# A fused RWKV-6 scan and SiLU feed-forward kernel: ScalarE's part of a weight piece, the odd-key copies, masks and block loads in another order

## The chip, the cores and the metric

The kernel runs on one core of a Trainium2 chip. The metric is device time in microseconds (us). A core has five engines that run side by side, each with its own queue: TensorE (PE in the profile), VectorE (DVE), ScalarE (ACT), GpSimd (POOL) and SyncE (SP), which here issues almost all transfers. [...] In this kernel the program sets the order in each queue by the order in which it emits instructions; nothing is rescheduled.

## The reference

Two blocks follow each other. The first is an RWKV-6 attention with a decaying state for each head, over 4 batches, 8 heads, 768 tokens and head size 48; the second is a feed-forward block with SiLU, 3072 tokens, width 384, inner width 2048.

```python
# r, k, v, w: (B, H, S, D) = (4, 8, 768, 48); u: (H, D)
for t in range(S):
    cur = einsum('bhd,bhe->bhde', u[None] * k[:, :, t], v[:, :, t])
    y[:, :, t] = einsum('bhd,bhde->bhe', r[:, :, t], state + cur)
    state = w[:, :, t, :, None] * state + einsum('bhd,bhe->bhde', k[:, :, t], v[:, :, t])
x = y.transpose(0, 2, 1, 3).reshape(B * S, H * D)      # (3072, 384)
h = x @ w_in                                           # (384, 2048)
out = (h / (1 + exp(-h))) @ w_out                      # (2048, 384)
```

r, k, v, w and u come as 32-bit floats. The two weight matrices come as 64-bit floats, and the kernel turns them into 32-bit floats itself.

## The kernel before

The tokens are cut into 12 units of 128 tokens and two batches. The scan of one unit runs in 7 levels, in which blocks of 1, 2, 4 ... 64 tokens meet their neighbours. At each level TensorE computes scores from r and the keys; VectorE keeps the scores of the level through a mask and decays r; GpSimd decays the keys for the next level; ScalarE copies the odd key blocks, which the level leaves as they are.

```python
def level(i, l):
    c, ni = 1 << l, L >> (l + 1)
    x_at, next_at = X[l % 2], X[(l + 1) % 2]          # two places for the level's keys
    if l + 1 < NL:
        nc.scalar.copy(out=keys(next_at * L + c, ...), in_=keys(NP * L + c, ...))  # odd keys, L384
    sc = [ps.tile([128, Q, L // 2], F32, name=name, bufs=2) for e in range(2)]     # p_sc (or p_h in unit 0)
    for p in range(NP):
        for e in range(2):
            nc.tensor.matmul(...)                     # scores, L396: lhsT=tk at x_at, rhs=tr
    def keep(e): nc.vector.copy_predicated(out=score..., mask=masks[l]..., data=sc[e]...)   # L405
    if not alone:                                     # alone: unit 0
        keep(0); keep(1)
    if l + 1 < NL or units[i][0] > 0:
        nc.vector.tensor_tensor(out=rb..., in0=rb..., in1=t..., op=ALU.mult)       # decay of r, L414
    if alone:
        keep(0); keep(1)
    for b in range(NB):
        nc.gpsimd.tensor_tensor(out=out, in0=have, in1=odd, op=ALU.mult)           # key products, L434
    if i < NTOK:                                      # units 0 and 1
        product(i, l)                                 # GpSimd: decays of the next level, L338
    add_weight()                                      # GpSimd: add of a joined weight piece, L206
```

The 64-bit weights come in 16 pieces of 256 columns or rows (0 to 7: w_in, 8 to 15: w_out). ScalarE takes a head (L174, L180) and tails into PSUM (L178); VectorE joins them with the rest of the words (L194, L196); GpSimd adds head and low part into the 32-bit weight (L206). Head and low part have two buffers each, the tails two PSUM tiles `p_o`. Pieces are loaded into staging places that earlier pieces must have left.

```python
def split_weight(i):                                  # ScalarE
    nc.scalar.activation(out=upper, in_=staged(i)..., func=AF.Abs)                 # L174
    tails = [ps.tile([128, DM], F32, name="p_o", bufs=2) for x in range(PW // DM)]
    for x, tail in enumerate(tails):
        nc.scalar.activation(out=tail, ..., func=AF.Copy, scale=8.0)               # L178
    nc.scalar.activation(out=head, in_=upper.bitcast(U16), func=AF.Relu, ...)      # L180
def round_weight(i):
    add_weight()
    if rounded and 0 < i <= 2 * NW:
        join_weight(i - 1)                            # VectorE: four instructions
    if rounded and i < 2 * NW:
        split_weight(i)
    for j in due.get(i, ()):
        load_weight(j)
```

The other steps that the prediction speaks of are: `turn` (a unit's w, r or k transposed), `turn_k` (its final keys transposed; the ScalarE copies are `kq`), `y` (the unit's output; copies `yt`), `dense_x` (output to feed-forward input; copies `xt`), `update` (the state, with copies by VectorE), `up(i, m)` (one of 8 tiles of `x @ w_in` and its Silu; PSUM tile `p_h`, two buffers), `down` and `quarter` (products with w_out), `sums` (VectorE sums of up tiles), `bonus`, `bonus_sum` and `bonus_write` (the term with u, which VectorE writes into the scores with two large copies, L368), `beat(n)` (n transposes of the identity that nobody reads, which keep TensorE busy). The order in which the start emits them:

```python
do((beat, 14), *both(bonus, 0), *both(bonus_sum, 0), (bonus_write, 0),
   *both(turn, 0, "k"), (beat, 8), *both(turn, 0, "r"), (beat, 4), *both(turn, 0, "w"), (level, 0, 0), (clear_state,),
   (make_mask, 4), (beat, 8), (level, 0, 1), (make_mask, 5), (beat, 8), (level, 0, 2), (make_mask, 6), (beat, 8),
   (level, 0, 3), (reverse_v, 0), (round_weight, 0), (beat, 6), (level, 0, 4), (clear_tokens,), (beat, 6), (level, 0, 5),
   *both(turn, 1, "w"), (clear, 0), (level, 0, 6))
blocks = block_loads(2)
do(*both(turn, 1, "r"), *blocks[:8], *both(turn_k, 0), *both(y_state, 0), *both(y, 0), (round_weight, 1),
   *both(dense_x, 0), *both(turn, 1, "k"), (reverse_v, 1), (round_weight, 2))
blocks = [*blocks[8:], (clear, 1), *block_loads(3)]
others = {0: both(update, 0) + both(bonus, 1), 3: [(bonus_sum, 1, 0)], 4: [(bonus_sum, 1, 1)], 5: [(bonus_write, 1)],
          6: [(load_values, 2), (load_rk, 2)]}
for l in range(NL):
    do((level, 1, l), (round_weight, 3 + l), (up, 0, l), *others.get(l, ()), *blocks[l * 3:l * 3 + 3])
do((up, 0, 7), *both(y_state, 1), *both(y, 1), (round_weight, 10), *both(dense_x, 1), (round_weight, 11),
   *both(turn_k, 1), *both(turn, 2, "w"), (products, 2), *both(update, 1))
turns = {1: both(turn, 2, "k"), 2: both(turn, 2, "r"), 3: [(reverse_v, 2)], 5: [(sums, 1, 0)]}
for m in range(6):
    do((round_weight, 12 + m), (up, 1, m), *turns.get(m, ()))
# ... then for each level l of unit 2: (level, 2, l), down or up steps, bonus, sums, block loads;
# from unit 3 on a fixed mixture of one scan with the feed-forward of the two units before it
```

Of the kernel before, what the change touches and what calls it, by code (L numbers as in the profile page):

```python
# [8 lines left out]
F32 = mybir.dt.float32  # L9
# [25 lines left out]
def kernel(  # L35
# [115 lines left out]
    due = {r: [] for r in range(-1, 2 * NW + 1)}  # L151
    for i in range(2 * NW):
        due[max([j + 1 for j in range(i) if rounded and PLACES[j] == PLACES[i]], default=-1)].append(i)
# [16 lines left out]
    def split_weight(i):  # L170
# [3 lines left out]
        nc.scalar.activation(out=upper, in_=staged(i).bitcast(BF16)[:, 3::4], func=AF.Abs)  # L174

        tails = [ps.tile([128, DM], F32, name="p_o", bufs=2) for x in range(PW // DM)]
        for x, tail in enumerate(tails):
            nc.scalar.activation(out=tail, in_=staged(i).bitcast(U16)[:, 2::4][:, x * DM:(x + 1) * DM],  # L178
                                 func=AF.Copy, scale=8.0)
        nc.scalar.activation(out=head, in_=upper.bitcast(U16), func=AF.Relu, scale=8.0 * 2.0 ** 16, bias=shift)  # L180
        half[i] = head, tails

    def join_weight(i):
        head, tails = half.pop(i)
        lo, hi = staged(i)[:, 0::2], staged(i)[:, 1::2]
        dst = w_ends[i][0].bitcast(U32)
        low = temps[:, 2, i % 2]

        def like(t):
            return t.rearrange("p (c f) -> p c f", c=dst.shape[1])  # L190

        for x, tail in enumerate(tails):
            part = slice(x * DM, (x + 1) * DM)
            nc.vector.scalar_tensor_tensor(out=tail.bitcast(U32), in0=lo[:, part], scalar=2.0 ** -29, in1=tail,  # L194
                                           op0=ALU.mult, op1=ALU.add)
            nc.vector.scalar_tensor_tensor(out=low[:, part], in0=hi[:, part], scalar=0x80000000, in1=tail.bitcast(U32),  # L196
                                           op0=ALU.bitwise_and, op1=ALU.bitwise_or)
        joined.append((dst, like(head), like(low)))
# [8 lines left out]

    def round_weight(i):

        add_weight()  # L210
        if rounded and 0 < i <= 2 * NW:
            join_weight(i - 1)
        if rounded and i < 2 * NW:
            split_weight(i)
        for j in due.get(i, ()):
            load_weight(j)
# [507 lines left out]
```

## Time and profile before

| what | value |
|---|---|
| time, median of 3 runs | 711.57 us (710.77 to 712.9) |
| span of the profiled execution | 709.6 us |
| TensorE busy | 673.4 us, 95% |
| TensorE weight loads busy | 591.4 us, 83% |
| VectorE busy | 437.8 us, 62% |
| GpSimd busy | 263.0 us, 37% |
| ScalarE busy | 186.4 us, 26% |
| transfers | 49.03 MB, mean 69 GB/s |

A line of a group names the line of the kernel, the engine, the operation and what it writes and reads. A line of the waits names the waiting instruction, the one that released it, then the total in us, how often, and the longest. A line of the timeline has start, duration, engine, line, operation, and in brackets the idle time just before and what ended it. The granted clock is TensorE's, as a share of full speed.

The start of the page's view in 40 slices (each 17.7 us) shows where TensorE is not full:

```
PE   6877967999999999999999999999999999999998
DVE  6857866579665665665665665666666667564131
ACT  5476575112022022022022022022022022021020
POOL 8838554525415414414414414423423524220000
```

### The profile page before, as it was taken

The page shows a single profiled execution, that of the slowest core. Times are in us where ns is not written, and L with a number is a line of the kernel's source. Part 1 is how long each engine was busy: PE and PEld are TensorE (multiplying, and loading weights), DVE is VectorE, ACT ScalarE, POOL GpSimd, SP SyncE. Part 2 cuts the span into 40 slices and gives each one's busy share as a digit, 9 for nine tenths or more (in the row PEclk, how much of TensorE's full clock was granted, in tenths as well). Part 3 has the DMA queues.
Part 4 walks back from the last instruction along what each step waited for, and adds up shares of the span by engine and source line. Part 5 has one row for each costly group of instructions (what it writes and reads, how often), then busy time and mean ns, then how long its engine had stood idle before and what let it go on. Part 6 is the DMA issues. An engine that isn't in the chain of part 4 may idle for free. (4 is left out here: it accounts for less than half of the span.)

```text
span 709.6 us, 12908 instructions
## 1 busy us (share of the span) xinstructions
PE 673.4 (95%) x4910; PEld 591.4 (83%) x4910; DVE 437.8 (62%) x777; ACT 186.4 (26%) x380; POOL 263.0 (37%) x372
## 2 busy tenths in 40 slices
PE   6877967999999999999999999999999999999998
PEld 5765756668989989989989989989989989889997
DVE  6857866579665665665665665666666667564131
ACT  5476575112022022022022022022022022021020
POOL 8838554525415414414414414423423524220000
PEclk9898998999999999999999999999999999999999
DMA  9937672432531441541541541540540300100000
GB/s 212 244 46 206 129 151 116 75 54 51 94 53 32 93 57 28 95 57 26 98 58 28 95 58 27 95 59 26 96 60 22 81 1 23 46 1 20 26 0 23
DMA packets 224237, 49.03 MB, mean 69 GB/s; under 512 B 212016, under 2 KB 219056, under 8 KB 224176
## 3 DMA queue, kind: packets, MB, share of 16 engines
q1 hardware_dynamic: 224032, 48.02, 34.6%
q8 instruction: 39, 0.64, 0.4%
q10 hardware_dynamic: 144, 0.20, 0.1%
q14 instruction: 22, 0.18, 0.1%
HBM read 39.52 MB, written 4.72 MB: 62 GB/s over the span
## 5 line engine op out<-in xcount | busy, mean ns | idle before, releaser
L555 PE MATMUL p_h<-xt,w_in_sb 128*128 128x256 f32 x1152 | 271.3, 390 | 6.6 <-ACT gt L561 4.4
L555 PEld LDWEIGHTS p_h<-xt,w_in_sb 128*128 128x128 f32 x1152 | 217.5, 193 | 42.0 <-ACT gt L561 5.2
L434 POOL TENSOR_TENSOR tk<-tk,tw 128x256 f32<-128x256 f32 x168 | 121.0, 742 | 201.3 <-PE p_sc L396 125.0
L405 DVE COPY_PREDICATED score<-mask,p_sc 128x512 f32<-128x512 int8 x162 | 133.6, 891 | 99.8 <-PE p_sc L396 99.7
L561 ACT ACTIVATE gt<-p_h 128x512 f32<-128x512 f32 x93 | 55.1, 594 | 254.6 <-PE p_h L555 254.6
L396 PEld LDWEIGHTS p_sc<-tr,tk 48*128 48x128 f32 x1296 | 80.1, 188 | 35.3 <-issue 25.8
L396 PE MATMUL p_sc<-tr,tk 48*128 48x128 f32 x1296 | 95.8, 286 | 10.5 <-POOL tk L434 4.0
L613 PE MATMUL p_o<-w_out_sb,gt 128*128 128x192 f32 x528 | 91.4, 330 | 0.0
L613 PE MATMUL p_o<-own,temps 128*128 128x192 f32 x528 | 90.8, 329 | 0.0
L613 PEld LDWEIGHTS p_o<-own,temps 128*128 128x128 f32 x528 | 85.4, 190 | 3.3 <-DVE partial L620 2.2
L613 PEld LDWEIGHTS p_o<-w_out_sb,gt 128*128 128x128 f32 x528 | 85.4, 190 | 2.0 <-issue 0.4
L414 DVE TENSOR_TENSOR tr<-tr,tw 128x512 f32<-128x512 f32 x82 | 68.2, 832 | 2.1 <-issue 1.3
L384 ACT COPY tk<-tk 128x256 f32<-128x256 f32 x72 | 32.7, 454 | 126.0 <-PE p_sc L396 108.8
L338 POOL TENSOR_TENSOR tw<-tw 128x512 f32<-128x512 f32 (+6 forms) x84 | 40.2, 478 | 51.6 <-DVE tw L306 46.9
L487 POOL TENSOR_TENSOR state<-state,tw 128x512 f32<-128x512 f32 x16 | 16.6, 1061 | 92.7 <-PE p_m L457 92.7
L595 DVE TENSOR_TENSOR temps<-gt 128x256 f32<-128x256 f32 x88 | 39.2, 445 | 17.3 <-ACT gt L561 16.9
L622 DVE TENSOR_TENSOR ob<-p_o,partial 128x192 f32<-128x192 f32 x44 | 15.6, 354 | 46.4 <-PE p_o L613 46.3
L496 DVE TENSOR_TENSOR state<-p_sc,state 48x384 f32<-48x384 f32 x16 | 8.9, 555 | 40.5 <-PE p_sc L482 40.4
L368 DVE COPY_PREDICATED score<-own_mask,diag 128x1024 f32<-128x1024 int8 x24 | 32.2, 1397 | 0.5
L613 PE MATMUL p_o<-w_out_sb,temps 128*128 128x192 f32 x176 | 30.4, 326 | 0.0
L613 PEld LDWEIGHTS p_o<-w_out_sb,temps 128*128 128x128 f32 x176 | 28.9, 190 | 0.0
L622 DVE TENSOR_TENSOR partial<-p_o,partial 128x192 f32<-128x192 f32 x33 | 11.6, 351 | 19.1 <-PE p_o L613 19.1
(91 smaller groups left out, 575.6 us busy)
## 6 DMA issues: line engine op xcount, KB each, us to landing
w_out_sb<-in_moe_w_in_dram SPq DMA_DIRECT2D x6, 768.0 KB, 6.8
out_dram<-ob SPq DMA_DIRECT2D x24, 192.0 KB, 1.9
tokens_rk<-in_r_dram SPq DMA_DIRECT2D x10, 384.0 KB, 3.8
tokens_rk<-in_k_dram SPq DMA_DIRECT2D x10, 384.0 KB, 5.2
w_out_sb<-in_moe_w_out_dram SPq DMA_DIRECT2D x4, 768.0 KB, 5.5
own<-in_moe_w_out_dram SPq DMA_DIRECT2D x4, 768.0 KB, 5.9
xt<-yt SPq DMA_DIRECT2D x60, 48.0 KB, 2.0
raw<-in_w_dram SPq DMA_DIRECT2D x80, 32.0 KB, 2.2
```

The source lines that it names most:

```text
L338: nc.gpsimd.tensor_tensor(out=up, in0=t[:, :, 0::2], in1=t[:, :, 1::2], op=ALU.mult)
L368: nc.vector.copy_predicated(out=score[:, i % NSC, e].rearrange("p (b q) t -> p b q t", b=NB), mask=own_mask[:, :, None, :].to_broadcast([1 ...
L384: nc.scalar.copy(out=keys(next_at * L + c, [4 * c, NP * ni // 2], [c, 2], [1, c]), in_=keys(NP * L + c, [4 * c, NP * ni // 2], [NP * L + c ...
L396: nc.tensor.matmul(bass.AP(tensor=s_p.tensor, offset=s_p.offset, ap=[s_p.ap[0], [apart * L // 2, 2], [1, L // 2]]), lhsT=tk[i][rows, x_at ...
L405: nc.vector.copy_predicated(out=dst, mask=masks[l][:, :, None].to_broadcast([128, NB, NP, ni, c]), data=sc[e].rearrange("p (b q) (i c) -> ...
L414: nc.vector.tensor_tensor(out=rb[:, :, :, 1, :], in0=rb[:, :, :, 1, :], in1=t[:, :, 0::2][:, :, :, None].to_broadcast([128, Q, ni, c]), op ...
L434: nc.gpsimd.tensor_tensor(out=out, in0=have, in1=odd, op=ALU.mult)
L555: nc.tensor.matmul(p_h[:, a, :], lhsT=w_in_sb[:, c, f * 128:(f + 1) * 128], rhs=xt[i][:, c, :], start=(c == 0), stop=(c == KC - 1))
L561: nc.scalar.activation(out=gt[i, m], in_=p_h, func=AF.Silu)
L595: nc.vector.tensor_tensor(out=out, in0=one, in1=two, op=op)
L613: nc.tensor.matmul(p, lhsT=left(f), rhs=right[:, f, :], start=(f == 0), stop=(f == FH - 1))
L622: nc.vector.tensor_tensor(out=to, in0=p, in1=known, op=ALU.add)
```

## The change

ScalarE's part of a piece is split in two, `head_weight` and `tail_weight`, and is emitted after the Silu of the cycle rather than before it. The copy of the odd keys for the next level is emitted at the end of a level, ahead of what follows in ScalarE's queue. Masks 4 to 6 of unit 0 move behind the key products that do not need them, and the bonus copies of unit 0 move between its levels 2 and 4. `clear` writes half as much (the other half stays zero). Unit 0's state update moves in front of unit 1's turn of k. Each cycle of unit 1's scan emits two groups of block loads instead of three, so that the loads of weight pieces stand earlier in SyncE's queue. The numbers of dummy transposes change.

```diff
-    def split_weight(i):
-        head = temps[:, 0, i % 2]
-        ...
+    def head_weight(i):
+        ...
         upper = temps[:, 1, i % 2].bitcast(BF16)[:, 0:PW]
         nc.scalar.activation(out=upper, in_=staged(i).bitcast(BF16)[:, 3::4], func=AF.Abs)
+        nc.scalar.activation(out=head, in_=upper.bitcast(U16), func=AF.Relu, scale=8.0 * 2.0 ** 16, bias=shift)
+    def tail_weight(i):
+        half[i] = [ps.tile([128, DM], F32, name="p_o", bufs=2) for x in range(PW // DM)]
+        for x, tail in enumerate(half[i]):
+            nc.scalar.activation(out=tail, ..., func=AF.Copy, scale=8.0)
     def join_weight(i):
+        add_weight()
         ... (the same four VectorE instructions)
+        for j in due.get(i, ()):
+            load_weight(j)
-    def round_weight(i): ...
     def clear(i):
-        clear_all(raw[...].rearrange("p (g d) -> p g d", d=32)[:, :, D - 32:32])
+        room = raw[...].rearrange("p (g d) -> p g d", d=32)
+        clear_all(room[:, 0::2, D - 32:32])
     def level(i, l):
-        if l + 1 < NL:
-            nc.scalar.copy(...)
+        def odd_keys(l): ... nc.scalar.copy(...)
+        if l == 0:
+            odd_keys(0)
         ... scores, keeps, decay of r, key products
+        if l + 2 < NL:
+            odd_keys(l + 1)
         if i < NTOK:
             product(i, l)
         add_weight()
@@ the order of the start
-    do((beat, 14), *both(bonus, 0), *both(bonus_sum, 0), (bonus_write, 0),
+    do((beat, 14), *both(bonus, 0), *both(bonus_sum, 0),
        *both(turn, 0, "k"), (beat, 8), *both(turn, 0, "r"), (beat, 4), *both(turn, 0, "w"), (level, 0, 0), (clear_state,),
-       (make_mask, 4), (beat, 8), (level, 0, 1), (make_mask, 5), (beat, 8), (level, 0, 2), (make_mask, 6), (beat, 8),
-       (level, 0, 3), (reverse_v, 0), (round_weight, 0), (beat, 6), (level, 0, 4), (clear_tokens,), (beat, 6), (level, 0, 5),
-       *both(turn, 1, "w"), (clear, 0), (level, 0, 6))
+       (beat, 20), (level, 0, 1), (beat, 8), (make_mask, 4), (level, 0, 2), (bonus_write, 0, [0]),
+       (beat, 8), (make_mask, 5), (make_mask, 6), (level, 0, 3), (bonus_write, 0, [1]), (head_weight, 0), (tail_weight, 0),
+       (beat, 8), (level, 0, 4), (reverse_v, 0), (clear_tokens,), (beat, 8), (level, 0, 5), *both(turn, 1, "w"), (clear, 0),
+       (level, 0, 6), (head_weight, 1))
-    do(*both(turn, 1, "r"), *blocks[:8], *both(turn_k, 0), *both(y_state, 0), *both(y, 0), (round_weight, 1),
-       *both(dense_x, 0), *both(turn, 1, "k"), (reverse_v, 1), (round_weight, 2))
+    do(*both(turn, 1, "r"), *blocks[:8], *both(turn_k, 0), *both(y, 0), (join_weight, 0), (tail_weight, 1),
+       *both(dense_x, 0), (reverse_v, 1), (join_weight, 1), *both(update, 0), *both(turn, 1, "k"), (head_weight, 2),
+       (tail_weight, 2))
-    blocks = [*blocks[8:], (clear, 1), *block_loads(3)]
-    others = {0: both(update, 0) + both(bonus, 1), 3: [(bonus_sum, 1, 0)], 4: [(bonus_sum, 1, 1)], 5: [(bonus_write, 1)],
-              6: [(load_values, 2), (load_rk, 2)]}
+    blocks = [*blocks[8:], *block_loads(3)]
+    others = {0: both(bonus, 1), 1: [(clear, 1)], 2: [(bonus_sum, 1, 0)], 3: [(bonus_sum, 1, 1)], 4: [(bonus_write, 1)]}
     for l in range(NL):
-        do((level, 1, l), (round_weight, 3 + l), (up, 0, l), *others.get(l, ()), *blocks[l * 3:l * 3 + 3])
-    do((up, 0, 7), *both(y_state, 1), *both(y, 1), (round_weight, 10), *both(dense_x, 1), (round_weight, 11),
-       *both(turn_k, 1), *both(turn, 2, "w"), (products, 2), *both(update, 1))
+        do((level, 1, l), (join_weight, 2 + l), (up, 0, l), (head_weight, 3 + l), (tail_weight, 3 + l),
+           *others.get(l, ()), *blocks[l * 2:l * 2 + 2])
+    do((up, 0, 7), *both(y, 1), (join_weight, 9), *both(dense_x, 1), (head_weight, 10), (tail_weight, 10), *both(turn_k, 1),
+       (join_weight, 10), *both(turn, 2, "w"), (products, 2), *both(update, 1), (head_weight, 11), (tail_weight, 11))
-    turns = {1: both(turn, 2, "k"), 2: both(turn, 2, "r"), 3: [(reverse_v, 2)], 5: [(sums, 1, 0)]}
-    for m in range(6):
-        do((round_weight, 12 + m), (up, 1, m), *turns.get(m, ()))
+    others = {0: [(load_values, 2)], 1: [(load_rk, 2)], 2: both(turn, 2, "k"), 3: both(turn, 2, "r"), 4: [(reverse_v, 2)]}
+    for m in range(5):
+        do((join_weight, 11 + m), (up, 1, m))
+        if m < 4:
+            do((head_weight, 12 + m), (tail_weight, 12 + m))
+        do(*others[m])
+    do((add_weight,), (up, 1, 5), (sums, 1, 0))
-    loads = block_loads(4)
+    loads = [*blocks[14:], *block_loads(4)]
```

## The prediction

> **What bounds the kernel now.** I first cut the span into stretches. The columns after the stretch's length are the busy times of TensorE (PE), its weight loads, VectorE (DVE), ScalarE (ACT) and GpSimd (POOL), then the granted clock, the DMA share and GB/s.
>
> ```profile
> 0.00:125.00 125.00, 94.93 (x710) 78.57 (x710) 90.84 (x153) 77.46 (x141) 78.49 (x113) 0.92 0.70 157
> 125.00:300.00 175.00, 172.94 (x1282) 147.64 (x1278) 116.24 (x194) 31.38 (x71) 68.39 (x93) 1.00 0.37 64
> 300.00:700.00 400.00, 399.29 (x2893) 359.26 (x2890) 229.43 (x426) 77.53 (x170) 116.11 (x166) 1.00 0.25 45
> ```
>
> From 125 us on TensorE is busy 572.2 of 575 us, at clock 1.00. The change leaves every matmul there in its order, so no saving can come from there. In the first 125 us TensorE lacks 30.1 us, and its clock is 0.92. This is the start: unit 0's scan alone, unit 1's scan beside the sixteen weight pieces, and then the hand-over to unit 2. Next I asked what TensorE waited for there (total, times, longest):
>
> ```profile
> PE p_h L555 <- ACT gt L561: 4.4, 1, 4.4
> PE p_sc L396 <- POOL tk L434: 4.0, 4, 1.7
> PE p_h L396 <- DVE tr L414: 3.3, 1, 3.3
> PE p_m L506 <- ACT yt L472: 3.1, 1, 3.1
> ...
> PE p_sc L482 <- ACT kq L444: 2.3, 1, 2.3
> PE p_h L555 <- POOL w_in_sb L206: 2.1, 2, 1.2
> PE p_sc L396 <- DVE state L498: 2.1, 1, 2.1
> ```
>
> There is no one bound: each engine in turn is the late one. Behind most of these waits stands ScalarE, which itself is stuck behind a weight piece (same view, ScalarE, 44 to 125 us):
>
> ```profile
> ACT p_o L178 <- DVE temps L196: 17.5, 12, 3.9
> ACT temps L174 <- DMA own<-in_moe_w_out_dram: 4.2, 1, 4.2
> ACT temps L180 <- POOL w_in_sb L206: 3.7, 3, 2.0
> ```
>
> Level 2 of unit 1 shows it in the timeline (start, duration). The odd-key copy L384 stands behind a piece's head, a Silu and a 1.46 us clear; GpSimd's products start as the copy ends (the view names no releaser for their 3.25 us), and TensorE, at 65.68, waits for these:
>
> ```profile
> 61.12 0.94 ACT L180 ACTIVATE temps<-temps,shift 128x768 uint32<-128x768 uint16 x1 [0.93 <-POOL w_in_sb L206]
> 61.96 0.58 ACT L561 ACTIVATE own<-p_h 128x512 f32<-128x512 f32 x1
> 62.44 1.46 ACT L319 COPY raw<-zero 128x1536 f32<-128x1536 f32 x1
> ...
> 63.80 0.40 ACT L384 COPY tk<-tk 128x256 f32<-128x256 f32 x1
> ...
> 64.33 1.29 POOL L434 TENSOR_TENSOR tk<-tk,tw 128x256 f32<-128x256 f32 x2 [3.25 <-issue]
> ```
>
> The longest single wait: a piece whose load has not landed stands in ScalarE's queue before a Silu, and TensorE wants that Silu's PSUM buffer:
>
> ```profile
> 110.47 0.88 ACT L174 ACTIVATE temps<-own 128x768 bf16<-128x768 bf16 x1 [4.19 <-DMA own<-in_moe_w_out_dram]
> 113.57 10.55 PE L555 MATMUL p_h<-xt,w_in_sb 128*128 128x256 f32 x36 [4.38 <-ACT gt L561]
> ```
>
> [...] at 61 to 64 us a copy whose data were ready waited behind three others. [...] Here the 110 to 120 us stretch, after the 4.4 us wait, has clock 0.66, and its 36 matmuls took 10.55 us against 8.36 us for the 36 before. [...] the pair of key products took 3.37 us at 13.25 us beside the two bonus copies, and 1.65 us at 125.4 us in unit 2.
>
> **The change, part by part.** I roll the start forward by hand with the durations of the timeline before: levels' scores 1.16 us and a pair of up tiles 2.86 us on TensorE; a keep pair 1.3 us (2.5 at levels 0 and 1), the decay of r 0.7 to 1.2, a join 2.25 on VectorE; a piece's ScalarE part 2.62 (0.91+0.94+0.96 less overlap); key products 1.25 to 1.9 and the piece's add 1.82 on GpSimd; a mask 1.35; the four bonus products 4.1.
>
> *Unit 0.* The two bonus copies (12.81 to 15.96) no longer stand before the first decay of r, which started at 15.85 and released TensorE at 17.31. The decay can start at 13.05. The key products then end it, at 13.25 + about 2.2 (my choice between 1.65 and 3.37) = 15.5, and 20 dummy transposes at 0.135 run to 15.7. Mask 4 moves behind the products of level 1 (level 2: 21.3 to 18.3), but masks 5 and 6 now stand together before level 3's products, 2.7 to 3.1 us: level 4 goes from 28.2 to 26.6 only. The ScalarE part of piece 0 then stands before odd copy 5: level 6 from 32.5 to 31.3. Here 1.2 us is in hand. But the head of piece 1 (1.8 us) now precedes the copies of unit 1's r, while the halved clear gives 0.75 back (1.49 to 0.75). So unit 0's key transposes start at about 35.0 against 35.2: the gain is spent. Without that head between yt and xt, xt is ready 0.5 earlier, which the state update's 0.9 us, moved in front of the turn of k, takes back: unit 1's level 0 at 44.8, as before.
>
> *Unit 1's scan.* Level 1 no longer waits for the state copy (52.7 to 50.2). Level 2 does not gain by it: GpSimd has product, add and four bonus products before level 1's key products, ending at 58.8 in both. From there the odd copy goes ahead of Silu, piece and clear, so level 2's products start at about 61.2 instead of 64.3. Cycles then are VectorE's, 1.3 + 0.8 + 2.25 = 4.35 us, against 6.9, 6.4, 3.9 and 5.2 before. In order, start of scores before and after:
>
> level 3: 65.7, 64.0; level 4: 72.1, 68.1; level 5: 76.0, 72.2; level 6: 81.2, 79.4 (the bonus copies, 2.5 to 4.1 us, now stand before level 5's keeps); unit 1's output y: 87.6, 86.2 (its last up tile waits for the add of piece 7); its yt copies: 92.5, about 88.
>
> From 84.4 to 91.6 us ScalarE before was in piece 9, whose tails waited 3.9 us for join 8 on VectorE (behind the bonus copies and the last keeps); the last two Silus and yt stood behind it, and so came the 3.1 us wait of L506. Now the bonus copies are done earlier, and join 8 follows the last keeps at about 83. The update of unit 1 comes at 95.5 instead of 99.9, the first up of unit 1 at 96.4 instead of 100.8: 4.4 us.
>
> *Six up tiles of unit 1.* TensorE needs 6 x 2.86 = 17.2 us; it took 23.2 with the 4.4 us wait and the half clock. The Silu now precedes each piece's head, and four weight loads stand 15 or so DMA issues (0.55 us each) earlier, so the 4.2 us wait on a load should go. I reckon some 2.5 us of other waits (ScalarE's head of piece 12 behind the GpSimd add of piece 10, itself behind the 3.5 us of unit 2's products). Unit 2's level 0 starts at 116.1 instead of 124.05.
>
> *Hand-over.* VectorE is then late: join 15, the sums of unit 1 and the keeps of level 0 end at about 124.5, so level 1 of unit 2 starts there instead of at 130.5. The gain that stays is 6.0 us. Each step assumes that things meet without slips, so I take off a tenth or so: 5.5 us, 711.57 - 5.5 = 706.
>
> *Steady state.* Odd copies at the end of a level stand before the Silus there too. TensorE waited for neither after 125 us, so this is worth 0; the block loads that move by one level likewise.
>
> **Rivals.** *VectorE is the bound already.* It is busy 35.0 of 43 us from 45 to 88 us, and the change removes none of its work. For it: my cycles end on VectorE. Against: it idled 9.5 us in that scan for scores that came late. If the keeps and bonus copies stretch by contention, about 3 us of gain are left: 708.5. *A copy that waits now blocks the Silus.* The odd copy needs GpSimd's products of its own level, and in level 1 these end at 58.8, long after up tile 1 is done; the first r copies stand behind a head. For it: the old order had the Silu ready earlier. Against: TensorE has two PSUM buffers for up tiles and waited for a Silu only once. With this and a lost unit 0: 711 to 713. *Nothing is lost at the hand-over.* If VectorE catches up, 8 to 10 us stay: 702 to 703. *A weight load comes later.* Loads still wait for joins; if pieces 13 or 15 land late, 4 us go again: 710.
>
> **Range and chances.** The four cases spread from 702 to 713; I hold most on 703 to 710, with 701 to 711 for 8 in 10. To be faster by over 2% takes 14.2 us, nearly half of all TensorE idle time at the start, which VectorE's work alone hardly allows: 0.05. Slower by over 2% would need 14 us more waits: 0.02. Within 2%: 0.93.
>
> **What would show it.** After: the same busy TensorE and clock 1.00 from 125 us on; TensorE's idle time in the first 125 us down from 30 to about 23; no wait for the state copy or for a Silu behind a load; level 2 of unit 1 still near 58.8 and levels 3 to 5 about 4 us apart; unit 2's level 0 near 116 and its level 1 near 124 with a wait for VectorE between them. I am wrong if unit 1's level 0 is over 1 us later than 44.8, if level 6 is not before 80.5, or if the span after unit 2's level 1 changes by more than 1 us.

## The result and the profile after

| | before | after |
|---|---|---|
| time, median | 711.76 us (710.77 to 712.9) | 718.32 us (716.62 to 719.25, 4 runs) |
| ratio to before, 95% interval | 1 | 1.0089 (1.0064 to 1.0113) |
| span of the profiled execution | 709.6 us | 717.2 us |
| mean granted clock over the span | 0.985 | 0.976 |

The kernel is slower by 6.6 us; 706.0 us with a range of 701 to 711 had been predicted. The same three stretches of the kernel after, with the columns explained in the prediction:

```profile
0.00:125.00 125.00, 99.23 (x709) 82.68 (x710) 84.24 (x144) 75.99 (x138) 78.54 (x112) 0.88 0.70 155
125.00:300.00 175.00, 168.80 (x1237) 143.23 (x1236) 120.53 (x199) 32.59 (x72) 70.70 (x93) 0.99 0.36 62
300.00:700.00 400.00, 399.02 (x2901) 358.07 (x2900) 229.90 (x429) 80.06 (x171) 120.28 (x168) 1.00 0.25 46
```

In the first 125 us TensorE is now busy for 99.2 us instead of 94.9, and yet it is further behind: it has done no more matmuls (709 records against 710), at a mean clock of 0.88 instead of 0.92. A busier TensorE that does the same work is a slower TensorE. In the second stretch it lacks 4 us more than before, which will turn out to be one wait. The third is unchanged, as predicted.

What TensorE waited for in the first 140 us of the kernel after (total, times, longest):

```profile
PE p_sc L397 <- DVE tr L415: 8.6, 3, 4.3
PE p_sc L397 <- POOL tk L435: 7.9, 4, 4.3
PE p_h L559 <- POOL w_in_sb L211: 2.8, 2, 1.6
...
PE p_h L559 <- ACT gt L565: 1.2, 2, 1.0
```

The lines have moved: L397 is the scores (L396 before), L415 the decay of r, L435 the key products, L559 the up tiles, L565 the Silu. Three of the waits of before are gone: the Silu behind a weight load (4.4 us, now no Silu wait over 1.0), the one for yt (3.1 us), and the one for the state copy (2.1 us). So the change did what it was for. In their place stand three waits of the scores of 4.1 to 4.3 us: one on the key products and two on the decay of r.

ScalarE's own waits between 44 and 125 us say the same. The 17.5 us behind joins and the 4.2 us for a load have become

```profile
ACT tk L382 <- POOL tk L435: 6.4, 2, 4.1
ACT p_o L185 <- DVE temps L199: 3.4, 2, 2.8
```

The up tiles of unit 1 run through. Six of them took 23.2 us before with one 4.38 us wait in the middle; in the timeline after, the first four are one unbroken group, and the last two wait 0.16 and 1.01 us:

```profile
106.38 12.31 PE L559 MATMUL p_h<-xt,w_in_sb 128*128 128x256 f32 x48
```

From its start to unit 2's level 0, at 125.51, are 19.1 us.

**The first new wait, unit 0's level 4.** Timeline after, start and duration, with lines of VectorE, GpSimd and TensorE:

```profile
21.87 1.31 DVE L365 COPY_PREDICATED score<-own_mask,diag 128x1024 f32<-128x1024 int8 x1
21.89 1.52 POOL L334 TENSOR_TENSOR tw<-tw 128x128 f32<-128x128 f32 x1
23.36 0.20 POOL L264 MEMSET mask<- 128x128 int8 x1
...
25.57 1.17 POOL L270 TENSOR_SCALAR_AFFINE_SELECT mask<-mask 128x64 int8<-128x64 int8 x1
...
27.21 1.23 POOL L435 TENSOR_TENSOR tk<-tk,tw 128x256 f32<-128x256 f32 x2
...
28.50 2.08 PE L397 MATMUL p_sc<-tr,tk 48*128 48x128 f32 x16 [4.32 <-POOL tk L435]
```

GpSimd needs from 21.89 to 28.4 us for one decay product, two masks and a pair of key products. The two masks alone are 23.36 to 27.2 us: 3.85 us. The scores then run at half clock: 16 matmuls in 2.08 us instead of 1.16, and the granted clock from 28.5 to 38.0 us is 0.50. In the kernel before, the same decay product ran beside a keep (24.19 to 25.49 on VectorE) and took a quarter of the time:

```profile
24.76 0.39 POOL L338 TENSOR_TENSOR tw<-tw 128x128 f32<-128x128 f32 x1
```

**The second, unit 1's level 6.** Same view:

```profile
82.14 4.11 DVE L365 COPY_PREDICATED score<-own_mask,diag 128x1024 f32<-128x1024 int8 x2
82.17 2.93 POOL L211 TENSOR_TENSOR w_in_sb<-temps 128x768 uint32<-128x768 uint32 x1 [1.11 <-DVE diag L363]
...
86.15 1.30 DVE L406 COPY_PREDICATED score<-mask,p_sc 128x512 f32<-128x512 int8 x2
87.36 0.67 DVE L415 TENSOR_TENSOR tr<-tr,tw 128x512 f32<-128x512 f32 x1
...
88.18 2.08 PE L397 MATMUL p_sc<-tr,tk 48*128 48x128 f32 x16 [4.25 <-DVE tr L415]
```

The two bonus copies stand in VectorE's queue before the keeps and the decay of level 5, and level 6's scores need that decay. Again half clock follows: scores of 2.08 us, and a granted clock of 0.50 from 88.2 to 90.2 us.

**The third, unit 2's level 1,** after the hand-over:

```profile
127.37 1.81 POOL L211 TENSOR_TENSOR w_out_sb<-temps 128x768 uint32<-128x768 uint32 x1 [1.86 <-DVE temps L199]
127.63 1.83 DVE L599 TENSOR_TENSOR temps<-gt 128x256 f32<-128x256 f32 x1
129.14 2.02 POOL L435 TENSOR_TENSOR tk<-tk,tw 128x256 f32<-128x256 f32 x2
129.57 0.88 DVE L599 TENSOR_TENSOR temps<-temps,gt 128x256 f32<-128x256 f32 x1
130.37 1.06 DVE L599 TENSOR_TENSOR temps<-gt 128x256 f32<-128x256 f32 x1
131.35 1.25 DVE L599 TENSOR_TENSOR temps<-gt,temps 128x256 f32<-128x256 f32 x1
132.53 2.43 DVE L406 COPY_PREDICATED score<-mask,p_sc 128x512 f32<-128x512 int8 x2
134.76 1.29 DVE L415 TENSOR_TENSOR tr<-tr,tw 128x512 f32<-128x512 f32 x1
136.19 1.25 PE L397 MATMUL p_sc<-tr,tk 48*128 48x128 f32 x16 [4.14 <-DVE tr L415]
137.38 6.99 PE L572 MATMUL p_o<-w_out_sb,gt 128*128 128x384 f32 x16
```

The four sums (L599) take 1.83 + 0.88 + 1.06 + 1.25 = 5.02 us. Before, they took 0.71 + 0.43 + 0.42 + 0.42 = 1.98 us, and were done about when level 0's scores began (124.05). Only the first of them had GpSimd at work beside it; from 122.69 to 125.39 GpSimd was idle. Timeline before:

```profile
120.88 1.81 POOL L206 TENSOR_TENSOR w_out_sb<-temps 128x768 uint32<-128x768 uint32 x1 [0.87 <-DVE temps L196]
122.27 0.71 DVE L595 TENSOR_TENSOR temps<-gt 128x256 f32<-128x256 f32 x1 [1.53 <-ACT gt L561]
123.08 0.43 DVE L595 TENSOR_TENSOR temps<-temps,gt 128x256 f32<-128x256 f32 x1
123.42 0.42 DVE L595 TENSOR_TENSOR temps<-gt 128x256 f32<-128x256 f32 x1
123.76 0.42 DVE L595 TENSOR_TENSOR temps<-gt,temps 128x256 f32<-128x256 f32 x1
```

The 16 down matmuls after the wait took 6.99 us, against 5.43 us for the same 16 before; the granted clock from 137.4 to 140.5 us is 0.50.

### The profile page after: what moved, and what is told of

Its sections match the earlier page's. It is cut to its first block, busy times and chain, and to the rows that moved or that the text cites. A ratio compares the mean times of both kernels' runs of the same rounds, so it can differ in the third digit from the quotient of the medians.

```text
span 717.2 us, 12925 instructions
## 1 busy us (share of the span) xinstructions
PE 680.9 (95%) x4926; PEld 597.5 (83%) x4926; DVE 437.1 (61%) x777; ACT 188.6 (26%) x380; POOL 269.5 (38%) x372
## 5 line engine op out<-in xcount | busy, mean ns | idle before, releaser
L559 PE MATMUL p_h<-xt,w_in_sb 128*128 128x256 f32 x1152 | 272.8, 392 | 3.9 <-POOL w_in_sb L211 2.8
L559 PEld LDWEIGHTS p_h<-xt,w_in_sb 128*128 128x128 f32 x1152 | 218.4, 194 | 39.9 <-POOL w_in_sb L211 3.2
L435 POOL TENSOR_TENSOR tk<-tk,tw 128x256 f32<-128x256 f32 x168 | 124.3, 763 | 168.7 <-PE p_sc L397 128.7
L397 PEld LDWEIGHTS p_sc<-tr,tk 48*128 48x128 f32 x1296 | 81.8, 192 | 45.2 <-issue 20.2
L397 PE MATMUL p_sc<-tr,tk 48*128 48x128 f32 x1296 | 97.7, 291 | 19.9 <-DVE tr L415 10.3
L565 ACT ACTIVATE gt<-p_h 128x512 f32<-128x512 f32 x93 | 55.2, 594 | 197.3 <-PE p_h L559 197.3
L415 DVE TENSOR_TENSOR tr<-tr,tw 128x512 f32<-128x512 f32 x82 | 65.1, 793 | 6.6 <-PE p_sc L397 4.4
L599 DVE TENSOR_TENSOR temps<-gt 128x256 f32<-128x256 f32 x88 | 41.0, 466 | 15.8 <-ACT gt L565 15.3
L348 POOL TENSOR_TENSOR ruk<-ruk,u_bc 128x384 f32<-128x384 f32 x22 | 22.6, 1029 | 1.7
```

What stands on the lines that cost most here:

```text
L348: engine.tensor_tensor(out=ruk[i, b], in0=ruk[i, b], in1=u_bc, op=ALU.mult)
L397: nc.tensor.matmul(bass.AP(tensor=s_p.tensor, offset=s_p.offset, ap=[s_p.ap[0], [apart * L // 2, 2], [1, L // 2]]), lhsT=tk[i][rows, x_at ...
L415: nc.vector.tensor_tensor(out=rb[:, :, :, 1, :], in0=rb[:, :, :, 1, :], in1=t[:, :, 0::2][:, :, :, None].to_broadcast([128, Q, ni, c]), op ...
L559: nc.tensor.matmul(p_h[:, a, :], lhsT=w_in_sb[:, c, f * 128:(f + 1) * 128], rhs=xt[i][:, c, :], start=(c == 0), stop=(c == KC - 1))
L565: nc.scalar.activation(out=gt[i, m], in_=p_h, func=AF.Silu)
L599: nc.vector.tensor_tensor(out=out, in0=one, in1=two, op=op)
```

## The experiments

My theory after reading this: each of the three waits comes from one place in the order, each costs its own length and then a stretch of half clock, and taking all three away gives the predicted path. The rival: VectorE is the bound in unit 1's scan, so that what is won at one place is lost at the next. Each of the first four kernels is the kernel after with one thing changed. Times are medians; ratios are to the kernel before, run beside them.

**Clock or wait?** Thirty more dummy transposes fill the time in which TensorE waits for the masks:

```diff
-       (beat, 8), (level, 0, 4), (reverse_v, 0), ...
+       (beat, 38), (level, 0, 4), (reverse_v, 0), ...
```

> The changed kernel with 30 more dummy transposes in unit 0 ahead of level 4, in TensorE's 4.3 us wait for the key products; no wait is removed. Theory (the clock): the wait itself was nearly as long before as a set of smaller ones; what costs is the half clock after it, which makes five batches 0.9 us longer each. Then unit 0's level 4 stays near 28.5 us, levels 5 and 6 come at about 31 and 33.5 instead of 32.4 and 36.3, unit 1's level 0 near 46.5 instead of 49.8, and the time falls by 2.5 to 4.5 us, to about 715. Rival (the wait, or ScalarE's new order): the clock costs nothing that lasts, and the time stays at 718 within 0.7 us.

Measured: 716.58 us (714.57 to 719.62, 9 runs), ratio 1.0075 (1.0052 to 1.0098). TensorE's timeline of this kernel:

```profile
23.00 4.37 PE L653 MATMUL p_m<-ident 128*128 128x128 f32 x38
28.45 1.16 PE L397 MATMUL p_sc<-tr,tk 48*128 48x128 f32 x16 [1.08 <-POOL tk L435]
29.54 1.09 PE L653 MATMUL p_m<-ident 128*128 128x128 f32 x8
```

Level 4 starts at 28.45, in effect where it did (28.50): the masks still delay it. But level 4's scores and the dummy transposes behind them now take 1.16 and 1.09 us, where after had 2.08 and 1.97, and the mean granted clock over the first 125 us is 0.96 instead of 0.88. Unit 0's key transposes come at 37.46 instead of 40.10 and unit 1's level 0 at 47.16 instead of 49.80: 2.6 us were the clock alone. At the end 1.7 us of them are left, less than the theory asked, and the intervals of the two ratios overlap, so the gain is shown in the trace and not in the time. The waits of 4.24 us at unit 1's level 6 and of 4.13 us at unit 2's level 1 stand as before.

**The masks.** Each one goes behind a pair of key products, in GpSimd's queue:

```diff
-       (beat, 8), (make_mask, 5), (make_mask, 6), (level, 0, 3), (bonus_write, 0, [1]), ...
-       (beat, 8), (level, 0, 4), ..., (beat, 8), (level, 0, 5), *both(turn, 1, "w"), ...
+       (beat, 8), (level, 0, 3), (bonus_write, 0, [1]), ..., (make_mask, 5),
+       (beat, 8), (level, 0, 4), ..., (beat, 8), (level, 0, 5), (make_mask, 6), *both(turn, 1, "w"), ...
```

> The changed kernel with mask 5 made after level 3's key products and mask 6 after level 5's, instead of both before level 3's products. Theory (masks in GpSimd's queue): the 4.3 us wait and the half clock after it go together; level 4 of unit 0 starts near 24.7 us, unit 1's level 0 at 43 to 45, and the time falls by 4 to 7 us, to 711 to 714. Rival (the head of piece 1 ahead of unit 1's r copies holds unit 0's end): level 4 moves, but unit 1's level 0 stays above 47 and the time falls by less than 2 us.

Measured: 714.41 us (712.12 to 716.0, 20 runs), ratio 1.0039 (1.0026 to 1.0052). Level 4 starts at 25.11, the key transposes at 35.03 and unit 1's level 0 at 44.73; I had predicted 26.6, 35.0 and 44.8 for the kernel after. The masks thus cost 5.1 us at unit 1's level 0 (49.80 less 44.73): 2.6 of clock by the run above, and 2.4 of delay. Of the 5.1 us, 3.9 reach the end.

**The bonus copies of unit 1** go back to where they were, behind level 5:

```diff
-    others = {..., 4: [(bonus_write, 1)]}
+    others = {..., 5: [(bonus_write, 1)]}
```

> The changed kernel with unit 1's bonus copies back at level 5, behind the keeps, the decay of r and the join, instead of ahead of level 5's keeps. Theory: the 4.1 us of copies no longer stand before the decay of r that TensorE's level 6 waits for; level 6 of unit 1 follows level 5 by about 4.5 us instead of 8.2, no half clock after it, and unit 1's output comes some 3 us earlier; the time falls by 2 to 4.5 us. Rival (VectorE is the bound in any order): the copies then delay the last keeps and joins by as much, and the time changes by less than 1 us.

Measured: 717.47 us (715.8 to 717.78, 4 runs), ratio 1.0074 (1.0045 to 1.0103), so 0.9 us less than after, within the intervals of both. In the profile level 6 follows level 5 after 4.7 us (79.75 to 84.47) instead of 8.2 (79.97 to 88.18), and the wait is 0.77 us, on a Silu. But the copies, now at 86.64 and again 4.12 us long, stand beside GpSimd's add of the last piece of w_in (from 86.66, 2.92 us instead of 1.82), and the last up tile waits 1.21 us for that weight. Unit 2's level 0 is 2.7 us earlier (122.84), level 1 as well (133.52, still with 4.14 us of wait). The rival's number, a change of less than 1 us, is met; its reason is half right: part of the 3.7 us won at level 6 is lost to the same copies one place further on.

**The sums** of unit 1 go behind unit 2's level 0 in VectorE's queue:

```diff
-    do((add_weight,), (up, 1, 5), (sums, 1, 0))
+    do((add_weight,), (up, 1, 5))
...
-    others = {0: both(bonus, 2) + [(load_rk, 3)], ...
+    others = {0: both(bonus, 2) + [(load_rk, 3), (sums, 1, 0)], ...
```

> The changed kernel with the first sums of unit 1's up tiles after level 0 of unit 2 instead of before it. Theory: at the hand-over TensorE waits 4.1 us for the decay of r, which stands on VectorE behind the sums (4.9 us with what they wait for); now the keeps and the decay come first, level 1 of unit 2 follows level 0 by 6 to 7 us instead of 10.7, the half clock after it goes too, and the time falls by 4 to 6 us, to 712 to 714. Rival (VectorE is late with the weight joins in any case): the keeps start when the joins end, and the time falls by less than 2 us.

Measured: 711.99 us (710.3 to 713.04, 12 runs), ratio 1.0002 (0.9984 to 1.0021). This one move takes back nearly the whole loss, 6.3 us. Its timeline:

```profile
126.97 2.46 DVE L406 COPY_PREDICATED score<-mask,p_sc 128x512 f32<-128x512 int8 x2
129.24 0.72 DVE L415 TENSOR_TENSOR tr<-tr,tw 128x512 f32<-128x512 f32 x1
129.88 1.05 DVE L599 TENSOR_TENSOR temps<-gt 128x256 f32<-128x256 f32 x1
```

The decay ends at 129.96, and level 1 comes 6.5 us after level 0 (124.86, 131.33), as in the kernel before; after needed 10.7. The sums still take 1.05 to 1.24 us each, but nobody waits for them.

The same move in the kernel **before**, as a control:

> The kernel before with only the first sums moved behind unit 2's level 0. Theory: there the weight joins end early enough (VectorE idled 1.5 us ahead of the sums), so nothing changes: 711.3 us within 0.8. Rival (the old place of the sums cost time in both kernels): 1.5 us or more faster.

Measured: 711.49 us (709.46 to 712.58, 12 runs), ratio 0.9998 (0.9979 to 1.0017). Nothing, as expected: there the sums were done before the keeps of level 0 could start (125.27) and stood in nobody's way. What had changed by the traces is when VectorE is free: its last join ended 3.3 us ahead of level 0's scores before (120.74 against 124.05), and 1.7 us behind their start after (127.22 against 125.51).

**All three** on top of the kernel after:

> The changed kernel with all three amendments: masks 5 and 6 behind key products, unit 1's bonus copies at level 5, the sums after unit 2's level 0. Theory (three waits ate the gain of the new ScalarE order): unit 2's level 0 near 116.5 us, as in the prediction, its level 1 some 6.5 us later near 123 instead of 130.5 in the kernel before, and 703 to 707 us: faster than the kernel before by 4 us or more. Rival (VectorE is the bound at the hand-over whatever is moved): level 1 of unit 2 near 129 to 130, and 709 to 712.

Measured: 705.62 us (705.27 to 707.3, 5 runs), ratio 0.9927 (0.9898 to 0.9956). The single moves sum to 3.9 + 0.9 + 6.3 = 11.1 us, together they give 12.7. Run once more as the base of two kernels below:

> The kernel with the masks behind the key products, the bonus copies of unit 1 at level 5 and the sums behind unit 2's keeps, once more, as the base for the next two: 705.6 us (704 to 707.5), unit 2's level 0 at about 118 us, its level 1 at about 124.6.

Measured: 705.15 us (703.97 to 706.62, 6 runs), ratio 0.9907 (0.9881 to 0.9933). Its path, beside the predicted one (starts of TensorE's scores, us):

| | predicted | after | after with all three moved |
|---|---|---|---|
| unit 0 level 4 | 26.6 | 28.50 | 25.21 |
| unit 1 level 0 | 44.8 | 49.80 | 44.83 |
| level 2 | 58.8 | 63.94 | 59.00 |
| level 3 | 64.0 | 71.70 | 66.18 |
| level 5 | 72.2 | 79.97 | 74.36 |
| level 6 | 79.4 | 88.18 | 79.07 |
| unit 2 level 0 | 116.1 | 125.51 | 117.32 |
| unit 2 level 1 | 124.5 | 136.19 | 123.79 |
| time | 706.0 | 718.32 | 705.15 |

In the first of these two runs' profiles unit 1's level 0 was at 46.41, in the second at 44.83: the same instructions, but in the first the 16 matmuls of unit 0's level 5 took 1.94 us instead of 1.16. So a milestone is good to some 1.6 us, whatever its two decimals say.

**What stretches the sums?** First the same kernel with two more moves at the start: mask 4 is made with the first four, and the head of piece 1 goes behind join 0 instead of in front of unit 1's r copies.

```diff
-    for l in range(4):
+    for l in range(5):
...
-       (level, 0, 6), (head_weight, 1))
+       (level, 0, 6))
...
-    do(..., *both(y, 0), (join_weight, 0), (tail_weight, 1),
+    do(..., *both(y, 0), (join_weight, 0), (head_weight, 1), (tail_weight, 1),
```

> As the version with all three amendments, and besides mask 4 made with the first four, in GpSimd's 1.9 us wait ahead of level 0, and the head of piece 1 behind unit 1's r copies and unit 0's y instead of ahead of them. Theory: unit 0's chain of key products gets 1 us shorter and the 1.7 us wait for the r copies goes; unit 1's level 0 comes 1 to 2.5 us earlier and the time is 1 to 2.5 us below the other version. Rival: the head then holds up the xt copies by as much, and the two are equal within 0.7 us.

Measured: 703.69 us (701.81 to 705.29, 4 runs), ratio 0.9888 (0.9854 to 0.9923), an interval that overlaps that of the three moves alone. Unit 0's level 3 came at 20.86 us instead of 21.92, and the wait for the r copies (1.69 us) went. But level 6's scores then took 2.08 us instead of 1.16, and unit 1's level 0 came at 44.81, as in the base: neither theory nor rival is settled by this profile. Then, on top of it, GpSimd's bonus products of unit 2 go one level later, so that GpSimd has less to do beside the sums:

```diff
-    others = {0: both(bonus, 2) + [(load_rk, 3), (sums, 1, 0)], 2: ...
+    others = {0: [(sums, 1, 0)], 1: both(bonus, 2) + [(load_rk, 3)], 2: ...
```

> The fastest version so far (703.7 us), but GpSimd's four bonus products of unit 2, and the load behind them, stand one level later, so that GpSimd has nothing to do beside the sums of unit 1 once its key products of level 0 end at about 122.4 us. Theory (the sums were stretched by GpSimd working beside them): the first sum, beside the key products, still takes about 1.05 us, and the sums that start after 122.4 us take about 0.42 us instead of 1.05 to 1.23; the time does not change by more than 1 us, as TensorE waits for nothing there. Rival (the sums are slow at this place for another reason, such as their data or the transfers under way): all four stay at 1.0 to 1.25 us.

Measured: 702.44 us (701.67 to 702.92, 4 runs), ratio 0.9875 (0.9849 to 0.9901). Timeline:

```profile
117.87 2.19 POOL L435 TENSOR_TENSOR tk<-tk,tw 128x256 f32<-128x256 f32 x2
...
119.28 1.07 DVE L599 TENSOR_TENSOR temps<-gt 128x256 f32<-128x256 f32 x1
120.44 0.42 DVE L599 TENSOR_TENSOR temps<-temps,gt 128x256 f32<-128x256 f32 x1
120.60 1.75 POOL L435 TENSOR_TENSOR tk<-tk,tw 128x256 f32<-128x256 f32 x2 [0.54 <-ACT tk L382]
120.79 0.96 DVE L599 TENSOR_TENSOR temps<-gt 128x256 f32<-128x256 f32 x1
121.67 0.95 DVE L599 TENSOR_TENSOR temps<-gt,temps 128x256 f32<-128x256 f32 x1
```

I had missed that the key products of level 1 follow at once when the bonus products no longer stand before them; GpSimd was idle only from 120.06 to 120.60. But that shows the cause more sharply than planned. The second sum started in this gap, 0.16 us before the next key products, and took 0.42 us. The sums on either side, with GpSimd at work, took 1.07, 0.96 and 0.95. All four have the same shape. They do not all read the same tiles, but that does not make the difference: with GpSimd idle, in the kernel before, the last three took 0.43, 0.42 and 0.42.

This kernel is the fastest of all, 1.25% under the kernel before. I don't credit the 1.2 us over the last one to the later bonus products: its profile was already 2.2 us ahead at unit 1's level 0 (42.58 against 44.81), before anything that this edit touches. Unit 0's level 6 took 1.16 us here and 2.08 there, and the mean granted clock of the profiled run was 0.998 here and 0.988 there.

**The odd copies.** Alone, on the kernel before:

```diff
-        if l + 1 < NL: (copy of the odd keys, at the start of level l)
+        if l == 0: odd_keys(0)
...
+        if l + 2 < NL: odd_keys(l + 1)          # at the end of level l
```

> The kernel before with only the odd-key copies moved to the end of the level. Theory: the copy leaves the queue behind Silu, piece and clear, so unit 1's level 3 comes 1.5 to 3 us before 65.7 us; the later Silus and the 4.2 us wait for a weight load stay, so 709 to 711.5 us. Rival (a copy that waits for GpSimd blocks ScalarE's Silus and pieces): 712.5 or more.

Measured: 712.58 us (711.53 to 714.62, 20 runs), ratio 1.0014 (1.0001 to 1.0027); a gain had been expected, and it was the rival's number, 712.5 or more, that came. Levels 3 to 6 of unit 1 did become quicker, 66.71 to 79.38 us, which is 12.7 us against 15.5 before. It was lost again at the Silu behind a weight load. From ScalarE's and TensorE's timelines of this kernel:

```profile
113.45 0.88 ACT L174 ACTIVATE temps<-own 128x768 bf16<-128x768 bf16 x1 [7.84 <-DMA own<-in_moe_w_out_dram]
116.55 10.12 PE L561 MATMUL p_h<-xt,w_in_sb 128*128 128x256 f32 x36 [7.12 <-ACT gt L567]
```

The wait grew from 4.4 to 7.1 us. Some of that is not the copies' doing: in the control with only the sums moved, where everything up to this point is as before, the same wait took 5.77 us, because the load was issued and landed later. So the levels gain by the odd copies, and the profile puts the loss at the load, but how much of it the copies cause is not shown.

Taken out of the kernel with all three moved, so that the odd copies are back at the start of the next level:

> The same, but with each odd-key copy at the start of the next level, as in the kernel of before. Theory (the copy stuck behind Silu, piece and clear cost unit 1's levels 3 to 5): a wait for GpSimd's products returns at levels 3 and 4 of unit 1, level 6 comes 1 to 3 us later and the time is 1 to 3 us longer. Rival (VectorE's keeps and joins set the levels by now, and the piece's ScalarE part a cycle ahead has already cleared the way): level 6 within 0.7 us, the time within 0.7 us.

Measured: 706.06 us (705.37 to 707.21, 6 runs), ratio 0.992 (0.9894 to 0.9945): 0.9 us more than the base, with intervals that overlap. A wait of 0.8 us for the copy returns at unit 1's level 5 and its level 6 comes at 79.85 instead of 79.07. The rival was nearer: with the pieces' ScalarE part behind the Silu, little is left for the copy to be stuck behind.

**The block loads.** The same base, with three groups of block loads per cycle as before:

```diff
-           *others.get(l, ()), *blocks[l * 2:l * 2 + 2])
+           *others.get(l, ()), *blocks[l * 3:l * 3 + 3])
...
-    loads = [*blocks[14:], *block_loads(4)]
+    loads = block_loads(4)
```

> The same, but with three groups of block loads in each cycle of unit 1's scan, as in the kernel of before, instead of two. Theory (fewer loads in a cycle let the weight pieces land earlier): pieces 11 to 15 are asked for later, the up tiles of unit 1 wait for joins whose pieces have not landed, unit 2's level 0 comes 1 to 4 us later and the time is 1 to 4 us longer. Rival (VectorE's joins, and not the loads, set the up tiles): unit 2's level 0 stays within 0.7 us and the time within 0.7 us.

Measured: 705.75 us (704.66 to 706.25, 6 runs), ratio 0.9913 (0.9886 to 0.994): 0.6 us more, not to be told from none, and no wait for a weight load anywhere. So the smaller groups are not what cured the Silu. SyncE's queue shows what may have. Before, the last two weight loads, for pieces 13 and 15, stood behind the value and token loads of unit 2:

```profile
96.60 2.71 SPq L114 DMA_DIRECT2D vq<-in_v_dram  x4
...
99.85 3.04 SPq L119 DMA_DIRECT2D tokens_rk<-in_k_dram  x1
...
104.50 0.92 SPq L159 DMA_DIRECT2D own<-in_moe_w_out_dram  x2
```

In the kernel with the large groups, the same view has them the other way round:

```profile
98.98 4.90 SPq L159 DMA_DIRECT2D own<-in_moe_w_out_dram  x2
103.93 0.46 SPq L110 DMA_DIRECT2D vt<-in_v_dram  x1
```

The change moves those value and token loads from level 6 of unit 1's scan to behind unit 1's first two up tiles. Piece 13 is the one that ScalarE waited for before. Counted from unit 1's first up tile, its load was issued 3.7 us after it before (104.50, 100.83) and 0.1 us ahead of it here (98.98, 99.06); piece 15's was not earlier (4.2 us after it before, at 105.0, and 4.5 here, at 103.5). The head of piece 13 moved too: ScalarE came to it 5.4 us after the first up tile before (at 106.28) and 8.6 us after it here (107.68), as it now follows a Silu. Both moves work against the wait. This is read from the queues; neither the order of the loads nor the new order of heads and tails was run alone.

## Why the prediction was wrong

**Right: the mechanism of the change, and the stretches it leaves alone.** Unit 0's levels 1 and 2 came at 15.37 and 18.32 us, predicted 15.7 and 18.3. The wait for yt, the wait for the state copy and the Silu behind a load went, as said. From unit 1's y to its update I said 9.3 us and measured 8.6 (96.83 to 105.41); from its first up tile to unit 2's level 0 I said 19.7 and measured 19.1. From unit 2's level 2 to the end before took 572.6 us (709.6 less 136.99) and after 572.9 (717.2 less 144.30).

All three signs of being wrong that I had written down came: unit 1's level 0 was 5.0 us later than 44.8, level 6 came at 88.18 and not before 80.5, and the span after unit 2's level 1 changed by 1.9 us (579.1 to 581.0).

**Wrong, first step: "masks 5 and 6 now stand together before level 3's products, 2.7 to 3.1 us: level 4 goes from 28.2 to 26.6 only".** I took two masks at 1.35 us. The kernel before had already shown one at 1.81 (from 25.09 us), with a select of 0.72 in it. Here the two took 3.85, because one select of 0.24 us took 1.17 and another 0.61, and the decay product in front of them took 1.52 instead of the 0.39 that it took before (at 24.76), beside a bonus copy that the change had put there. I had allowed for a busy neighbour with the key products two lines above (3.37 us beside the bonus copies, 1.65 in unit 2) and not with these. Level 4 was late by 1.9 us; the rest of the 5.0 us by which unit 1's level 0 missed comes with the next step.

**Wrong, second step: the clock.** I noted the slow matmuls behind the wait that the change removes (10.55 us against 8.36) and rolled everything forward at full clock, although my own numbers held waits of several us where TensorE had nothing to do. In the profiles of the kernels before and after, with more dummy transposes, with the sums moved and with the odd copies alone, all nine waits of 4.1 us and more were followed by slow matmuls: scores of 2.08 us instead of 1.16, or the matmuls right behind them, such as 6.99 for 5.43. Behind the four of them before and after, the granted clock was 0.50 for at least 2 us (from 113.6 to 117.0 before, and from 28.5 to 38.0, 88.2 to 90.2 and 137.4 to 140.5 after). Waits of some 3 us went both ways. One of 3.26 us in the kernel before was followed by scores of 2.08 us (at 17.31, granted clock 0.51 to 23.2). Waits of 3.03 to 3.04 us at unit 1's level 2 were followed by scores of 1.51 us in the kernel with the large block loads, and of 1.16 in two others, where only the up tiles behind, after another 1.18 us of wait, were slow (4.35 and 4.40 for 2.86); behind the wait of 3.07 us for yt in the kernel before, the granted clock was 1.00 (93.1 to 96.1). That it is the wait that costs the clock was tested once, by filling the one in unit 0 (1.08 us of wait for 4.32, and scores of 1.16 us for 2.08). And several shorter waits close together went with half clock, 1.58, 1.35 and 1.18 us between 56 and 66 us in the kernel after, with groups of up tiles of 4.54 and 5.49 us instead of 2.86 (granted clock 0.50 from 66.3 to 71.7). The second of these lies between levels 2 and 3 of unit 1, where I had 5.2 us and 7.8 were measured: its 2.6 us are the difference. Over unit 0 the clock alone cost 2.6 us, by the run with more dummy transposes.

**Nearly right in size, wrong in weight: the bonus copies, "2.5 to 4.1 us".** They took 4.11. My own figure of 7.2 us from level 5 to level 6 met 8.2. What I did not do is look at that step as a wait: 7.2 us for a cycle in which TensorE has 4.0 us of work (1.16 and 2.86) is a wait of over 3 us, and slow matmuls follow (granted clock 0.73 from 88.2 to 96.8 us; from level 6 to y 8.7 us instead of the 6.8 I had).

**Wrong, third step: the hand-over, "join 15, the sums of unit 1 and the keeps of level 0 end at about 124.5".** That was 8.4 us after unit 2's level 0; it became 10.7. The order was right, the sizes were not. The prediction gives none for the sums; at the 0.42 us that they take with GpSimd idle, four are 1.7 us. In the new order they stand beside an add of 1.82 us and a pair of key products, and took 5.02; the decay took 1.29 instead of the 0.72 that it takes with the sums moved away. That is 3.9 of the 4.14 us of wait. The sums are VectorE instructions that now had GpSimd at work beside them, and the 0.42 against 0.95 to 1.07 us in one and the same kernel is the cleanest measurement of that here. I had allowed for such a neighbour in one row of the timeline only, that of the key products.

The sum of it, as lateness against the predicted path, each row from one profile and so no surer than the 1.6 us above:

| at | late by | what came in since the row above |
|---|---|---|
| unit 1 level 0 | 5.0 us | masks (2.4) and half clock in unit 0 (2.6), by the two runs |
| unit 1 level 3 | 7.7 | half clock in a group of up tiles (2.6) |
| unit 1 level 6 | 8.8 | bonus copies at the upper end (4.11) |
| unit 1 y | 10.6 | half clock after level 6 |
| unit 2 level 0 | 9.4 | 1.2 less than predicted for update, turns and up tiles |
| unit 2 level 1 | 11.7 | sums stretched at the hand-over |
| end | 12.3 | half clock in the down tiles (1.6), less 0.5 that I had taken off for slips and 0.9 by which the profiled run lies over the median; 0.4 is not accounted for |

Of the rivals, "VectorE is the bound already" had keeps and bonus copies stretch, and left 3 us of gain; it was nearer in kind but wrong in place: the keeps kept their 1.3 us, the bonus copies of unit 1 took 4.11 us as they had before (4.14), and it was the sums and GpSimd's own instructions that stretched. "A weight load comes later" did not happen in the kernel after. "A copy that waits now blocks the Silus" did, but cost nothing there: the odd copy of unit 1 at 63.92 us had waited 4.11 us for GpSimd with a Silu behind it, and the longest wait of an up tile for a Silu was 1.01 us. The predicted 705 to 706 us is what the change gives once three steps stand elsewhere; that the number is met then is partly luck, since the move of the sums also takes away 1.9 us of hand-over that I had booked as lost, and levels 3 to 5 were 2 us later than predicted.

## What to carry to other kernels

Before an order is changed, list for each moved instruction what the other of the pair VectorE and GpSimd does at its new place, and take its duration from a place where that neighbour is busy (a sum took 0.42 us when it started beside an idle GpSimd, and 0.95 to 1.07 beside a busy one). In these runs a hole of some 4 us in TensorE's queue cost its length plus half as much again or so (4.32 us of wait and 2.6 of clock, 4.14 and 1.6), and holes of 3.03 to 3.26 us were followed by scores of 1.16 to 2.08 us. Count a new one so, as an estimate, and fill it with dummy matmuls or, better, move what makes it behind the instruction that the next matmul waits for: masks behind key products, sums behind the decay. When a stretch gets faster, look at what the two stretches that now touch have in their queues; the sums cost nothing in the kernel before and 6.3 us in the one after.

## What the runs showed of the hardware that I had not expected

In the four overlaps below of a bonus copy on VectorE with an instruction on GpSimd, the one that started first was no longer than elsewhere (1.29 to 1.32 us for a copy, 1.31 in the median of its 24, and 1.82 for an add), and the one that started second was longer and ended later. Here are the two bonus copies of unit 1 in the view of their line (shortest, median and longest in ns, then the first and the last start), in the kernel after and in the kernel before, with GpSimd's add beside them before:

```profile
L365 DVE COPY_PREDICATED score<-own_mask,diag x2: 1319/2108/2898, 82.1 to 83.4; 128x1024 f32<-128x1024 int8 x2
L368 DVE COPY_PREDICATED score<-own_mask,diag x2: 1287/2119/2951, 82.7 to 85.5; 128x1024 f32<-128x1024 int8 x2
82.64 1.82 POOL L206 TENSOR_TENSOR w_in_sb<-temps 128x768 uint32<-128x768 uint32 x1
```

After, the copies start 0.03 us ahead of the add. As the pair ends at 86.25, the first copy, from 82.14, is the one of 1.32 us, and the second, from 83.4, that of 2.90. GpSimd's add starts at 82.17 and ends at 85.10. The add thus takes 1.11 us more than the 1.82 us that it takes at 90.37. It ends 1.64 us after the first copy, and the second copy ends 1.15 us after it. Before, the add starts 0.04 us ahead of the copies (82.64 and 82.68) and takes its 1.82 us, to 84.46; the first copy, from 82.68, is the one of 2.95 us and ends 1.17 us after the add, and the second, from 85.5, the one of 1.29. Why the one that starts second is longer, no run here shows.

Small GpSimd instructions that started just behind such a copy were longer too. The decay product at 21.89, which took 0.39 us before, ended 0.23 us after the bonus copy beside it (23.41, 23.18). The select at 25.57, of a kind that takes 0.24 us at most places, took 1.17 and ended 0.08 us after the bonus copy that had started 0.20 us ahead of it (26.74, 26.66). Both ended only once the copy had.
